# Block-sorted attention and a gated feed-forward on one Trainium2 core: the first two units' scores computed a second time transposed, later transposes by DMA, batch 0 in halves

## The chip, the core and the metric

One core of a Trainium2 chip runs the whole program. Its engines are TensorE (PE in the profile, its weight loads PEld), VectorE (DVE), ScalarE (ACT), GpSimd (POOL) and SyncE (SP), which only issues DMAs here; POOL issues the loads that turn fp32 into bf16. The metric is device time in microseconds (us), the median over runs. All times below are us unless a unit stands with them.

## What is computed

Inputs are q, k and v of 4 batches x 8 heads x 768 rows x 64, a matrix of 8x8 per head (sort_net), and three weight matrices (512x1536, 512x1536, 1536x512). All are fp32; the output is 3072x512, fp32.

```
P = sort_net
for _ in range(5):                      # per head, 8x8
    P = exp(P - max(P, axis=-1)); P = P / (sum over the row + 1e-9); P = P / (sum over the column + 1e-9)
k_sorted[i] = sum_j P[i, j] * k_block[j]        # blocks of 96 rows, the same for v
scores = q_block @ k_sorted_block.T / 8         # 96x96, block by block
attn   = exp(scores - rowmax); attn = attn / (rowsum + 1e-9)
x      = attn @ v_sorted_block                  # to 3072 tokens x 512
g = x @ w_gate
out = (g * sigmoid(g) * (x @ w_val)) @ w_out
```

## The kernel before

**Units.** Half a batch (4 blocks of 96 rows, all 8 heads) is a unit: 384 tokens, eight units. Heads are handled as four head pairs hp: head hp on partitions 0 to 63 and head hp+4 on 64 to 127 (x is 0 or 1).

**Preparation per batch.** q is loaded (line 92) and transposed on TensorE in three pieces of 16 transposes (q_piece, line 130). K is mixed by P and transposed in one step: `mix_t` (lines 134 to 143) multiplies K as it was loaded by a block-diagonal matrix bdk, made of P, in six pieces of 16 small matmuls. V of batches 1 to 3 is mixed by one 128x512 matmul a piece (v_piece, line 169), six a batch, and brought into the layout that attention needs through DRAM: written to vscr (line 177) and read back (line 179). V of batch 0 goes by `mix_t` and 32 TensorE transposes (v0_turn, line 160). ACT moves most pieces from PSUM to SBUF (evict, line 120).

**Attention of a unit, per head pair.** qk (line 251): eight matmuls into PSUM tile s (96x768). rowmax and shift on VectorE (lines 257, 262), expo on ACT (267), rowsum and reciprocal on VectorE (271, 272), norm on POOL (278), which gives en in bf16; turn (285): eight TensorE transposes of en, moved by ACT to et; av (298): eight matmuls with V, moved by ACT into xt, the input of the feed-forward part.

**Feed-forward (FFN) of a unit.** Twelve steps m, each for 128 of the 1536 hidden columns: four matmuls g and four u (line 318) of 128x384, tanh on ACT (328), gs = (tanh+1)*g and h = u/2*gs on VectorE (332, 338). Every third h of unit 0 goes another way: ACT copies u (335), POOL multiplies (336). ffn_down (346) turns three chunks of h into part of an output tile of 128x512; ACT copies it (350), SP stores it (351).

**Order.** The program is written in one order per engine by hand (manual_schedule). Up to the first FFN step it is a list (`first`, lines 399 to 404). From there each action has a time in slots, `at(t, ...)`, and is emitted in the order of these times: slot 12u+m holds step m of unit u's FFN, with a quarter of an output tile of unit u-1 at +0.5. The attention of unit u runs beside the FFN of the two units before: `att_steps` starts head pair hp at slot 12u-15.6+3hp, with turn 4 and av 5 slots later (lines 303 to 310). Batch 1 is prepared in unit 0's slots, batch 2 in slots 12 to 29, batch 3 in slots 36 to 53. Each engine takes its instructions strictly in that order, so a wait holds all that stands behind it.

**PSUM.** Eight banks: three rotate for g and u ("up"), one for output tiles ("o"), two for one score tile ("s"), two for all the rest ("m").

Of the kernel before, what the change touches and what calls it, by code (L numbers as in the profile page):

```python
# [9 lines left out]
FP32 = mybir.dt.float32  # L10
# [7 lines left out]
def kernel(  # L18
# [15 lines left out]

    nc = tc.nc
# [18 lines left out]
    CC = BLK // CQ  # L58

# [10 lines left out]
    dramp = ctx.enter_context(tc.tile_pool(name="dramp", bufs=2, space=bass.MemoryType.DRAM))  # L70
    psum = ctx.enter_context(tc.tile_pool(name="psum", bufs=2, space=bass.MemoryType.PSUM))

    def ps_tile(shape, dt, name, tag):
        return psum.tile(shape, dt, name=name, tag=tag, bufs={"up": 3, "o": 1, "s": 1, "m": 2}[tag])

    ctx.enter_context(tc.manual_schedule())


# [5 lines left out]
    def load_k(b):  # L84
        kn[b] = natp.tile([128, CK, D], BF16, name="kn", tag="kn", bufs=2)
        src = k[b].rearrange("h (j ch c) d -> (h j ch) c d", j=NB, ch=CH)
        nc.gpsimd.dma_start(out=kn[b], in_=src)

    def load_q(b):
        qn[b] = natp.tile([128, 2, CC, D], BF16, name="qn", tag="qn", bufs=2)  # L90
        src = q[b].rearrange("(x hp) (j cq c) d -> (hp j cq) x c d", x=2, j=NB, cq=CQ)
        nc.gpsimd.dma_start(out=qn[b], in_=src)

    def load_v(b):
        vn[b] = natp.tile([128, CK, D], BF16, name="vn", tag="vn", bufs=2)
        src = v[b].rearrange("h (j ch c) d -> (h j ch) c d", j=NB, ch=CH)
        nc.gpsimd.dma_start(out=vn[b], in_=src)
# [5 lines left out]

    p_sb = const.tile([BH, NB + 1, NB], FP32, name="p_sb")
    nc.sync.dma_start(out=p_sb[:, 0:NB, :], in_=sort_net.rearrange("b h i j -> (b h) i j"))
    load_q(0)
    load_k(0)
    load_v(0)
    load_w(wg_sb, moe_w_gate, 0, DF // 2)

    ident = const.tile([128, 128], BF16, name="ident")
    make_identity(nc, ident)
    load_w(wv_sb, moe_w_val, 0, DF // 2)

# [9 lines left out]
    def q_piece(b, n, eng, tag):  # L124
        if n == 0:
            tr["q", b] = trp.tile([128, HP, NB, BLK], BF16, name="qt", tag="qt")
        ps = ps_tile([128, 8, 128], BF16, "q_ps", tag)
        for l in range(8):
            for x in range(2):
                nc.tensor.transpose(ps[ds(64 * x, 64), l, :], qn[b][:, x, n * 8 + l, :], ident)  # L130
        dst = tr["q", b].rearrange("p hp i (cq c) -> p (hp i cq) c", cq=CQ)
        evict(eng, dst[:, :, ts(n, 8)], ps.transpose([0, 2, 1]))

    def mix_t(nat, b, dst, n, eng, tag):

        ps = ps_tile([128, 8, 64], FP32, "k_ps", tag)
# [330 lines left out]
```

## Time and profile before

| | |
|---|---|
| median of 3 runs (lowest to highest) | 286.16 (285.83 to 286.68) |
| profiled execution, first to last instruction (span) | 284.0 |
| around the span, median less span | 2.2 |
| first FFN matmul | 36.36 |
| first FFN matmul of units 1, 2, 3 | 66.10, 98.43, 128.41 |
| of units 4, 5, 6, 7 | 160.17, 190.15, 218.84, 246.59 |
| last output tile stored (issue) | 281.08 |
| loads that turn fp32 into bf16, in what lands | 14.16 MB |

The profiled execution's own time is given as its span only; what lies around the span is taken to be that of the median run. The profile's busy times of TensorE are those of pipelined matmuls whose ends are modelled, so the price of a group is read from the start of one to the start of the next. PEclk is the share of TensorE's full clock that was granted. Idle time of an engine that does not set the pace costs nothing. In a row of windows stand start and end, length, then busy time and count of PE, PEld, DVE, ACT and POOL, the granted clock, the share of time that the DMA engines were busy, and GB/s. In a row of the timeline: start, busy time, engine, line, operation, tiles written and read, shapes, count, and in brackets the wait before it.

### The profile page before, as it was taken

The numbers are of one execution on the slowest core, as the hardware profiler recorded it, in microseconds if no ns is written. First come the engines' busy times: TensorE is split into PE (matmuls) and PEld (weight loads), VectorE is DVE, ScalarE is ACT, GpSimd is POOL, SyncE is SP. The second block draws the span as 40 slices with busy tenths as digits, with TensorE's granted clock in tenths as the row PEclk, the third lists the DMA queues.
The fourth block names the chain that finished last, engine by engine and source line by source line (L and its number), as shares of the span: only waits on it lengthen the run. The fifth ranks groups of instructions, "written<-read, shape, count | busy, mean of one in ns | idle before, by whom it ended". The sixth has DMA issues, their size and how long they took to land.

```text
span 284.0 us, 6237 instructions
## 1 busy us (share of the span) xinstructions
PE 258.5 (91%) x2550; PEld 154.6 (54%) x2550; DVE 204.0 (72%) x360; ACT 164.3 (58%) x291; POOL 70.3 (25%) x98
## 2 busy tenths in 40 slices
PE   0577789989999999999999999999999999999983
PEld 0566645655556665555555655555555555555531
DVE  5789577749778777888887777888888887556500
ACT  2568779885766767546666666554555445432311
POOL 8155362433332222222211222222222222000000
PEclk9955589999999999999999999999999999999999
DMA  6999999997399911001039100101000010000021
GB/s 105 216 206 221 204 203 197 268 207 75 51 227 244 111 39 38 10 31 39 28 137 133 39 2 37 40 0 39 38 37 2 37 39 37 18 22 37 37 76 74
DMA packets 28412, 25.57 MB, mean 90 GB/s; under 512 B 19296, under 2 KB 22880, under 8 KB 28384
## 3 DMA queue, kind: packets, MB, share of 16 engines
q0 software_dynamic: 5968, 14.16, 26.7%
q1 hardware_dynamic: 22416, 11.02, 15.9%
q8 instruction: 20, 0.33, 0.5%
q14 instruction: 8, 0.07, 0.1%
HBM read 30.68 MB, written 8.65 MB: 138 GB/s over the span
## 4 chain that ended last, share of the span: by engine, by line
PE 65%; DVE 15%; ACT 12%; issue 4%; DMA 2%; DVEq 0%; ACTq 0%; POOLq 0%
PE o_ps L346 19%; PE g_ps L318 17%; PE u_ps L318 14%; DVE e L262 5%; DVE rm L257 5%; PE av_ps L298 3%; ACT et L120 3%; PE k_ps L139 3%; ACT e L267 3%; PE et_ps L285 2%; DMA qn<-in_q_dram 2%; ACT th L328 2%; PE s L251 2%; DVE gs L332 2%; DVE h L338 2%
## 5 line engine op out<-in xcount | busy, mean ns | idle before, releaser
L278 POOL TENSOR_TENSOR en<-e,rs 96x384 bf16<-96x384 f32 x63 | 50.9, 827 | 145.3 <-DVE rs L272 113.1
L332 DVE SCALAR_TENSOR_TENSOR gs<-th,g_ps 128x384 bf16<-128x384 bf16 x96 | 52.2, 544 | 42.5 <-ACT th L328 42.5
L346 PE MATMUL o_ps<-wo_sb,h 128*128 128x512 bf16 x288 | 76.8, 380 | 2.3 <-ACT o_sb L350 2.0
L318 PE MATMUL u_ps<-xt,wv_sb 128*128 128x384 bf16 x384 | 78.3, 327 | 0.6 <-DVE gs L332 0.5
L318 PE MATMUL g_ps<-xt,wg_sb 128*128 128x384 bf16 x384 | 78.8, 328 | 0.0
L328 ACT ACTIVATE th<-g_ps 128x384 bf16<-128x384 f32 x96 | 47.1, 490 | 53.9 <-PE g_ps L318 52.6
L338 DVE SCALAR_TENSOR_TENSOR h<-u_ps,gs 128x384 bf16<-128x384 f32 x92 | 51.3, 557 | 9.9 <-PE o_ps L346 0.5
L318 PEld LDWEIGHTS <-wg_sb 128*128 128x128 bf16 x384 | 36.9, 98 | 35.1 <-issue 2.0
L318 PEld LDWEIGHTS <-wv_sb 128*128 128x128 bf16 x384 | 37.7, 98 | 26.1 <-issue 1.6
L267 ACT ACTIVATE e<-e 96x768 f32<-96x768 f32 x32 | 27.0, 843 | 19.3 <-DVE e L262 19.3
L346 PEld LDWEIGHTS <-h 128*128 128x128 bf16 x288 | 23.9, 98 | 22.9 <-issue 3.1
L262 DVE TENSOR_TENSOR e<-s,rm 96x768 f32<-96x768 f32 x32 | 30.5, 954 | 2.8
L257 DVE TENSOR_REDUCE rm<-s 96x8 f32<-96x768 f32 x32 | 30.2, 943 | 2.8 <-PE s L251 2.7
L271 DVE TENSOR_REDUCE rs<-e 96x8 f32<-96x768 f32 x32 | 30.0, 938 | 1.3 <-ACT e L267 1.3
L120 ACT COPY et<-et_ps 96x768 bf16<-96x768 bf16 x32 | 25.0, 781 | 1.7 <-PE et_ps L285 1.7
L350 ACT COPY o_sb<-o_ps 128x512 f32<-128x512 f32 x24 | 14.0, 585 | 16.8 <-PE o_ps L346 16.7
L285 PEld LDWEIGHTS <-en 96*96 96x96 bf16 x256 | 17.4, 133 | 3.2
L285 PE MATMUL et_ps<-ident,en 96*96 96x96 bf16 x256 | 18.1, 217 | 0.0
L120 ACT CAST xt<-av_ps 128x384 bf16<-128x384 f32 x32 | 15.3, 477 | 4.4 <-PE av_ps L298 3.6
L130 PE MATMUL q_ps<-ident,qn 128*64 128x128 bf16 x192 | 8.5, 244 | 9.0 <-DMA qn<-in_q_dram 8.0
L298 PEld LDWEIGHTS <-vt 96*64 96x64 bf16 x256 | 9.4, 114 | 11.8 <-issue 11.3
L298 PE MATMUL av_ps<-et,vt 96*64 96x96 bf16 x256 | 12.2, 218 | 3.8 <-ACT et L120 3.3
(54 smaller groups left out, 154.3 us busy)
## 6 DMA issues: line engine op xcount, KB each, us to landing
out_dram<-o_sb SPq DMA_DIRECT2D x24, 256.0 KB, 2.0
qn<-in_q_dram POOLq DMA_DIRECT2D x4, 768.0 KB, 10.0
kn<-in_k_dram POOLq DMA_DIRECT2D x4, 768.0 KB, 10.4
vn<-in_v_dram POOLq DMA_DIRECT2D x4, 768.0 KB, 13.3
vscr<-vm SPq DMA_DIRECT2D x3, 768.0 KB, 6.7
vt<-vscr SPq DMA_DIRECT2D x3, 768.0 KB, 8.3
wg_sb<-in_moe_w_gate_dram POOLq DMA_DIRECT2D x4, 384.0 KB, 15.8
wv_sb<-in_moe_w_val_dram POOLq DMA_DIRECT2D x4, 384.0 KB, 18.1
```

The lines of the kernel that those rows point to most:

```text
L120: nc.scalar.copy(dst, src)
L257: nc.vector.reduce_max(m[:, :, :, 0], st["s", u, hp], axis=AX.X)
L262: nc.vector.tensor_tensor(e, st["s", u, hp], st["m", u, hp].to_broadcast([BLK, 2, HB, BLK]), op=ALU.subtract)
L267: nc.scalar.activation(st["e", u, hp], st["e", u, hp], AF.Exp, scale=scale)
L278: engs[x].tensor_tensor(st["en", u, hp][:, x], st["e", u, hp][:, x], st["rs", u, hp][:, x].to_broadcast([BLK, HB, BLK]), op=ALU.mult)
L285: nc.tensor.transpose(ps[:, x * HB + i, :], st["en", u, hp][:, x, i, :], ident[0:BLK, 0:BLK])
L298: nc.tensor.matmul(ps[ds(64 * x, 64), i, :], lhsT=tr["v", b][:, (x * HP + hp) * NB + i0 + i, :], rhs=st["et", u, hp][:, x, i, :], start=Tr ...
L318: nc.tensor.matmul(ps, lhsT=w_sb[:, kc, ts(m, 128)], rhs=xt[u][:, kc, :], start=(kc == 0), stop=(kc == HP - 1))
L328: nc.scalar.activation(st["th"], st["g"], AF.Tanh, scale=0.5)
L332: nc.vector.scalar_tensor_tensor(gs, st["th"], 1.0, st["g"], op0=ALU.add, op1=ALU.mult)
L338: nc.vector.scalar_tensor_tensor(h_t[u][:, m, :], st["u"], 0.5, gs, op0=ALU.mult, op1=ALU.mult)
L346: nc.tensor.matmul(st["o"], lhsT=h_t[u][:, m, ts(t, 128)], rhs=wo_sb[:, m, :], start=(m == 0), stop=(m == NFC - 1))
```

## The change

- **Scores of units 0 and 1 twice.** qk as before gives maxima (t_max, VectorE), which TensorE turns (t_maxt) and ACT copies; then t_st computes the scores again, transposed, and takes the maxima off by a second matmul with a constant matrix (selm); t_exp goes straight from PSUM to bf16 on ACT. Nothing is turned afterwards. The row sums are matmuls with ones (t_av), and t_div divides after av: reciprocal on VectorE, then the product on VectorE or, for two head pairs of unit 0 and all of unit 1, by an ACT copy and POOL. shift, rowsum, norm and turn fall away for these units.
- **Transposes by DMA.** From unit 2 on, turn is one DMA transpose from SP of en (padded to 128 columns a block). q of batches 2 and 3 is loaded in another layout by eight DMAs a batch (load_qd) and turned by four DMAs (qd_turn). V of batches 1 to 3 is mixed by 16 small matmuls a piece, as K is, and turned by two DMAs (v_flip); the way through DRAM is gone. V of batch 0 is still turned on TensorE. (v0_flip is defined and not called.)
- **Batch 0 in halves.** q is loaded in two halves of pieces of three rows; q, K and V are prepared for unit 0 first, K and V with matmuls half as wide and twice as many (mix_half, v0_piece); unit 1's K follows ahead of the first FFN step, its q and V in unit 0's slots.
- **Joined visits.** av of a head pair stands just ahead of qk of a later one in the same slot (6.05 and 0.1); a V and a K piece of batches 2 and 3 stand together, every third slot, in slots 16 to 31 and 40 to 55.
- **h over ACT and POOL.** Every second h up to step 8, then two of three, instead of every third in unit 0 alone (via_pool).
- **Banks.** PSUM banks are named by hand; the last three output tiles rotate over four banks ("oo ua ub uc"). Weights are loaded in thirds.

The diff, cut:

```diff
-    def ps_tile(shape, dt, name, tag):
-        return psum.tile(shape, dt, name=name, tag=tag, bufs={"up": 3, "o": 1, "s": 1, "m": 2}[tag])
...
+    sa = psum.tile([128, 2, 512], FP32, name="sa_ps")
+    bank = {n: psum.tile([128, 512], FP32, name=f"{n}_ps") for n in ("ma", "mb", "ua", "ub", "uc", "oo")}
...
+    def ps(group, shape, dt=FP32, parts=128):
+        turns[group] = turns.get(group, -1) + 1
+        names = group.split()
+        t = bank[names[turns[group] % len(names)]]
...
+    UP, MM = "ua ub uc", "ma mb"
...
+    def load_q0(half):
...
+    def load_qd(b, x):
+        if x == 0:
+            qd[b] = natp.tile([BLK, NB, HP, 2, D], BF16, name="qd", tag="qn", bufs=2)
+        for hp in range(HP):
+            nc.gpsimd.dma_start(out=qd[b][:, :, hp, x, :],
+                                in_=q[b][x * HP + hp].rearrange("(i c) d -> c i d", i=NB))
...
+    def q0_piece(half, n, eng, group):
...
+        for l in range(6):
+            hp, c = 2 * n + l // CC0, l % CC0
+            for x in range(2):
+                nc.tensor.transpose(p[ds(64 * x, 64), l, :], qn[0, half][:, x * HP + hp, c, :], ident)
...
+    def qd_turn(b, part):
...
+        n = NB // 4
+        nc.sync.dma_start(out=tr["qx", b][:, ts(part, n)].rearrange("p i hp c -> p (i hp) c"),
+                          in_=qd[b][:, ts(part, n)].rearrange("c i hp x d -> c (i hp x d)"),
+                          transpose=True)
+    def mix_half(nat, half, dst, n, eng, group):
+        p = ps(group, [16, 32])
+        for l in range(16):
+            for x in range(2):
+                nc.tensor.matmul(p[ds(64 * x, 64), l, :], lhsT=nat[:, n * 16 + l, :],
+                                 rhs=bdk[:, 0, ds(HP * x, HP), ds(half * HB, HB)],
+                                 start=True, stop=True)
+        evict(eng, dst[:, :, ts(n, 16)], p.transpose([0, 2, 1]))
...
-    def v_piece(b, n, eng, tag):
...
-        ps = ps_tile([128, 8, D], FP32, "v_ps", tag)
-        nc.tensor.matmul(ps.rearrange("p c d -> p (c d)"),
-                         lhsT=bdk[:, b].rearrange("p h i c -> p (h i c)"),
-                         rhs=vn[b][:, ts(n, 8), :].rearrange("p c d -> p (c d)"),
-                         start=True, stop=True)
-        evict(eng, tr["vm", b][:, ts(n, 8), :], ps)
-    def v_turn(b):
...
-        nc.sync.dma_start(out=scr.rearrange("hi (ch c) d -> (hi ch) c d", ch=CH), in_=tr["vm", b])
-        tr["v", b] = trp.tile([BLK, H * NB, D], BF16, name="vt", tag="vt")
-        nc.sync.dma_start(out=tr["v", b], in_=scr.rearrange("hi c d -> c hi d"))
...
+    def v0_piece(half, n, eng, group):
...
+        evict(eng, dst[:, :, :, ts(n, 16)], p.rearrange("p l (g ch) -> p g ch l", ch=CH))
+    def v_piece(b, n, eng, group):
...
+        p = ps(group, [8, 64])
+        for l in range(8):
+            for x in range(2):
+                nc.tensor.matmul(p[ds(64 * x, 64), l, :], lhsT=vn[b][:, n * 8 + l, :],
+                                 rhs=bdk[:, b, ds(HP * x, HP)].rearrange("p a i c -> p (a i c)"),
+                                 start=True, stop=True)
+        evict(eng, dst[:, :, :, ts(n, 8)], p.rearrange("p l (g ch) -> p g ch l", ch=CH))
+    def v0_turn(half, n, eng, group):
...
+        for g in range(8):
+            nc.tensor.transpose(p[:, g, :], vpad[:, half * 16 + n * 8 + g, 0:BLK], ident)
...
+    def v_flip(b, part, parts=2):
...
+        n = HP * NB // parts
+        nc.sync.dma_start(out=tr["vb", b][:, ts(part, n), :],
+                          in_=vpad[:, ts(part, n), :].rearrange("p g c -> p (g c)"), transpose=True)
...
+    def qk_mm(out, u, hp):
+        for i in range(HB):
+            for x in range(2):
+                r = ds(64 * x, 64)
+                nc.tensor.matmul(out[x][:, ts(i, BLK)], lhsT=tr["q", u][r, hp, i, :],
+                                 rhs=tr["k", u][r, hp, i, :], start=True, stop=True)
...
+    def t_qk(u, hp, pair):
+        st["s", u, hp] = [bank[n] for n in pair.split()]
+        qk_mm([t[0:BLK] for t in st["s", u, hp]], u, hp)
+    def halves(u, hp):
+        s = st["s", u, hp]
+        if s[0] is bank["na"]:
+            return [(slice(0, 2), sa[0:BLK, :, 0:UT])]
+        return [(slice(x, x + 1), s[x][0:BLK, 0:UT].unsqueeze(1)) for x in range(2)]
+    def t_max(u, hp):
+        m = rmb[hp]
+        for x, s in halves(u, hp):
+            nc.vector.reduce_max(m[:, x, 0:HB], s.rearrange("p x (i c) -> p x i c", i=HB), axis=AX.X)
+        st["m", u, hp] = m
+    def t_maxt(u, hp, eng):
+        p = st["s", u, hp][0][:, UT:UT + BLK // 2].bitcast(BF16)
+        nc.tensor.transpose(p, st["m", u, hp].rearrange("p x i -> p (x i)"), ident[0:BLK, 0:BLK])
+        mt = smp.tile([128, BLK], BF16, name="mt", tag="mt")
+        evict(eng, mt, p)
+        st["mt", u, hp] = mt
+    def t_st(u, hp):
+        for i in range(HB):
+            for last in range(2):
+                for x in range(2):
+                    r = ds(64 * x, 64)
+                    nc.tensor.matmul(st["s", u, hp][x][0:BLK, ts(i, BLK)],
+                                     lhsT=selm[r, i, :] if last else tr["k", u][r, hp, i, :],
+                                     rhs=st["mt", u, hp][r, :] if last else tr["q", u][r, hp, i, :],
+                                     start=not last, stop=bool(last))
+    def t_exp(u, hp):
+        et = epool.tile([BLK, 2, HB * BLK], BF16, name="ett", tag="ett", bufs=3)
+        for x, s in halves(u, hp):
+            nc.scalar.activation(et[:, x], s, AF.Exp, scale=scale)
+        st["et", u, hp] = et
+    def t_av(u, hp, av, den):
+        new_xt(u)
+        av, den = ps(av, [UT]), ps(den, [UT])
+        et = st["et", u, hp]
+        for x in range(2):
+            nc.tensor.matmul(den[ds(64 * x, 64), :], lhsT=ones, rhs=et[:, x, :], start=True, stop=True)
+        for i in range(HB):
+            for x in range(2):
+                nc.tensor.matmul(av[ds(64 * x, 64), ts(i, BLK)],
+                                 lhsT=tr["v", u][0:BLK, hp, i, ds(64 * x, 64)],
+                                 rhs=et[:, x, ts(i, BLK)], start=True, stop=True)
+        st["av", u, hp] = av, den
+    def t_div(u, hp, eng):
+        av, den = st["av", u, hp]
+        r = smp.tile([128, UT], FP32, name="rden", tag="rden", bufs=2)
+        nc.vector.reciprocal(r, den)
+        if eng == "dve":
+            nc.vector.tensor_tensor(xt[u][:, hp, :], av, r, op=ALU.mult)
+        else:
+            x = smp.tile([128, UT], FP32, name="xu", tag="xu", bufs=2)
+            nc.scalar.copy(x, av)
+            nc.gpsimd.tensor_tensor(xt[u][:, hp, :], x, r, op=ALU.mult)
+    ens = [epool.tile([BLK, 2 * HB, 128], BF16, name=f"en{n}", tag=f"en{n}", bufs=1) for n in range(3)]
...
+    def norm(u, hp):
+        en = ens[(u * HP + hp) % 3]
...
         for x in range(2):
...
+            nc.gpsimd.tensor_tensor(en[:, ds(x * HB, HB), 0:BLK], st["e", u, hp][:, x],
+                                    st["rs", u, hp][:, x].to_broadcast([BLK, HB, BLK]), op=ALU.mult)
     def turn(u, hp):
-        ps = ps_tile([BLK, 2 * HB, BLK], BF16, "et_ps", "m")
-        for x in range(2):
-            for i in range(HB):
-                nc.tensor.transpose(ps[:, x * HB + i, :], st["en", u, hp][:, x, i, :],
-                                    ident[0:BLK, 0:BLK])
...
+        et = epool.tile([128, 2 * HB, BLK], BF16, name="et", tag="et", bufs=3)
+        nc.sync.dma_start(out=et, in_=st["en", u, hp].rearrange("p g c -> p (g c)"), transpose=True)
         st["et", u, hp] = et
...
+        p = ps(MM, [HB, BLK])
...
+    def via_pool(u, m):
+        s = NFC * u + m
+        return s % 2 == 1 if s < 9 else s % 3 < 2 if s < 20 else s % 3 != 1
...
-            nc.scalar.activation(u_sb, st["u"], AF.Copy, scale=0.5)
-            nc.gpsimd.tensor_tensor(h_t[u][:, m, :], u_sb, gs, op=ALU.mult)
...
+        if via_pool(u, m):
...
+            nc.scalar.activation(st["us", u, m], st["u", u, m], AF.Copy, scale=0.5)
...
+    def ffn_h(u, m):
+        if via_pool(u, m):
+            nc.gpsimd.tensor_tensor(h_t[u][:, m, :], st["us", u, m], st["gs", u, m], op=ALU.mult)
...
-            st["o"] = ps_tile([128, DM], FP32, "o_ps", "o")
+            st["o"] = ps(group, [DM])
...
+    for n, (eng, b) in enumerate([("act", "oo"), ("dve", "ua"), ("act", "ub")]):
+        k0_piece(0, n, eng, b)
...
+    v0_piece(0, 0, "act", "ma")
+    v0_piece(0, 1, "act", "mb")
+    t_qk(0, 0, "na nb")
+    t_max(0, 0)
+    t_qk(0, 1, "ua ub")
+    t_max(0, 1)
+    t_qk(0, 2, "uc oo")
+    t_max(0, 2)
+    t_maxt(0, 0, "act")
+    v0_piece(0, 2, "act", "ma")
+    t_st(0, 0)
+    t_maxt(0, 1, "act")
+    t_exp(0, 0)
+    t_qk(0, 3, "ma mb")
+    t_max(0, 3)
+    t_st(0, 1)
+    t_maxt(0, 2, "act")
+    t_exp(0, 1)
+    v0_turn(0, 0, "dve", "na")
+    t_st(0, 2)
+    t_maxt(0, 3, "act")
+    t_exp(0, 2)
+    t_st(0, 3)
+    v0_turn(0, 1, "dve", "ua")
+    t_exp(0, 3)
+    t_av(0, 0, "ub", "uc")
+    t_div(0, 0, "pool")
+    t_av(0, 1, "na", "nb")
+    t_div(0, 1, "pool")
+    t_av(0, 2, "ua", "oo")
+    t_div(0, 2, "dve")
+    t_av(0, 3, "ma", "mb")
+    t_div(0, 3, "dve")
+    k0_piece(1, 0, "act", "uc")
+    k0_piece(1, 1, "act", "oo")
+    k0_piece(1, 2, "act", "na")
...
+    for t, f, args in [
+            (1.0, v0_piece, (1, 0)), (1.0, v0_piece, (1, 1)), (2.0, v0_piece, (1, 2)), (3.0, v0_turn, (1, 0)),
+            (5.0, v0_turn, (1, 1)), (4.0, k_piece, (1, 0)), (4.9, k_piece, (1, 1)), (5.0, k_piece, (1, 2)),
+            (6.0, k_piece, (1, 3)), (6.9, k_piece, (1, 4)), (7.0, k_piece, (1, 5)), (5.9, q_piece, (1, 0)),
+            (7.4, q_piece, (1, 1)), (8.0, q_piece, (1, 2)), (8.9, v_piece, (1, 0)), (9.0, v_piece, (1, 1)),
+            (9.9, v_piece, (1, 2)), (10.0, v_piece, (1, 3)), (10.4, v_piece, (1, 4)), (10.9, v_piece, (1, 5))]:
+        st["n"] = st.get("n", 0) + 1
+        at(t + 0.1, f, *args, ("act", "dve")[st["n"] % 2], P3 if t < 11.4 else MM)
+    for part in range(2):
+        at(11.2 + 0.1 * part, v_flip, 1, part)
+    for hp in range(HP):
+        t = 1 + 2 * hp
+        for dt, f, args in [(0.2, t_qk, ("na nb",)), (0.35, t_max, ()), (1.05, t_maxt, ("act",)), (1.2, t_st, ()),
+                            (1.95, t_exp, ()), (3.07, t_av, (P3, P3)), (3.35, t_div, ("pool",))]:
+            at(t + dt, f, 1, hp, *args)
...
+    for x in range(2):
+        at(20.0 + 4 * x, load_qd, 2, x)
+        at(41.0 + 4 * x, load_qd, 3, x)
...
+        t = 24 * b + T0
+        for n in range(6):
+            at(t - 16 + 3 * n + 0.05, v_piece, b, n, "act", MM)
+            at(t - 16 + 3 * n + 0.06, k_piece, b, n, "act", MM)
+        for part in range(2):
+            at(t + 0.1 * part, v_flip, b, part)
+        for part in range(4):
+            at(t - 6 + part, qd_turn, b, part)
+    for u in range(2, NU):
+        t0 = 12 * u + T0 + (u == 2)
+        for hp in range(HP):
+            for dt, f in [(0.1, qk), (0.35, rowmax), (0.45, shift), (1.6, expo), (2.1, rowsum), (2.12, recip),
+                          (2.3, norm), (2.4, turn), ((5.05 if u == 2 else 6.05) - 0.07 * (hp == 3), av)]:
+                at(t0 + 3 * hp + dt, f, u, hp)
...
-        at(12 * NU + t, ffn_down, NU - 1, t, 0, 1)
...
+        at(12 * NU + t, ffn_down, NU - 1, t, 0, 1, "oo " + UP)
```

## The prediction

> **What bounds the kernel.** The page's busy shares and slices come first:
>
> ```profile
> PE 258.5 (91%) x2550; PEld 154.6 (54%) x2550; DVE 204.0 (72%) x360; ACT 164.3 (58%) x291; POOL 70.3 (25%) x98
> ...
> PE   0577789989999999999999999999999999999983
> ...
> PEclk9955589999999999999999999999999999999999
> DMA  6999999997399911001039100101000010000021
> ```
>
> TensorE is full from about 36 us on, and before that neither full nor at its clock. The windows by unit, cut where the first g_ps matmul of each unit of the feed-forward part (FFN) starts, say how long each lasts:
>
> ```profile
> 36.36:66.10 29.74, 26.63 (x336) 16.41 (x335) 20.85 (x34) 23.55 (x43) 12.02 (x15) 0.97 1.16 214
> 66.10:98.43 32.33, 32.26 (x339) 18.63 (x338) 26.03 (x44) 21.57 (x41) 10.70 (x14) 1.00 0.81 145
> ...
> 190.15:218.84 28.69, 28.39 (x230) 16.20 (x228) 24.04 (x41) 15.03 (x27) 6.43 (x8) 1.00 0.08 29
> ```
>
> So units 1 to 6 are TensorE's own work; the units between last 29.98, 31.76, 29.98, and unit 6 27.75. The timeline of TensorE gives the price of each visit, read from start to start (busy times overlap):
>
> ```profile
> 191.45 0.52 PE L285 MATMUL et_ps<-ident,en 96*96 96x96 bf16 x8
> 191.81 0.81 PE L346 MATMUL o_ps<-wo_sb,h 128*128 128x512 bf16 x3
> 192.46 0.81 PE L318 MATMUL g_ps<-xt,wg_sb 128*128 128x384 bf16 x4
> 193.10 0.81 PE L318 MATMUL u_ps<-xt,wv_sb 128*128 128x384 bf16 x4
> 193.96 0.36 PE L298 MATMUL av_ps<-et,vt 96*64 96x96 bf16 x8
> 194.26 0.82 PE L346 MATMUL o_ps<-wo_sb,h 128*128 128x512 bf16 x3
> ```
>
> A slot (g, u and a third of o) is 3x0.65 = 1.95. The turn costs 0.36. av costs 0.30 and another 0.21 between u_ps and it (193.10 to 193.96 is 0.86, not 0.65); qk costs 0.31 and 0.09. Three slots with one head pair of attention: 5.85+0.36+0.51+0.40 = 7.12; the chain repeats at 7.13. The waits and the windows of the start show two more places:
>
> ```profile
> PE o_ps L346 <- ACT o_sb L350: 2.0, 3, 0.7
> ...
> 17.50:20.90 3.40, 2.42 (x74) 2.06 (x68) 2.68 (x4) 3.00 (x6) 2.44 (x4) 0.50 1.15 206
> ...
> 34.60:38.00 3.40, 3.40 (x30) 2.21 (x26) 2.57 (x4) 2.06 (x5) 1.53 (x2) 0.50 1.16 212
> 38.00:41.40 3.40, 2.51 (x21) 1.53 (x20) 2.56 (x5) 3.17 (x6) 1.63 (x3) 1.00 1.10 210
> ```
>
> The last tiles wait for one PSUM bank, and the clock stays at 0.50 from 14.1 on until TensorE was busy for 3.40 of 3.40 us.
>
> **Basis.** The span is 284.0; the median of the runs is 286.16, so 2.2 lie around it. The profiled execution has no other time; I sum from 284.0+2.2.
>
> **Units 1 to 7.** Units 2 to 7 of attention lose the turn (-0.36 each), batches 2 and 3 lose six q pieces (0.57 each, 59.98 to 60.55). Against that a V piece, one matmul of 0.22 (73.12 to 73.34), becomes 16 small ones like a K piece, 0.37 (83.35 to 83.73). Joining av and qk saves the 0.09 of the second visit. In qk right after av (88.56 to 88.86 is 0.30) there is no extra. So three slots become 5.85+0.21+0.30+0.31 = 6.67; a V and a K piece together, in a visit of their own, add 0.84. Head pair 3's av comes 0.07 slots early, ahead of the slot's g, so it isn't joined: 0.90, not 0.81.
> - Unit 1: 23.4 for 12 slots, five qk and four av (3x0.40+2x0.51+0.81+0.90 = 3.9), three V-K visits (2.5): 29.9, by 2.4 less.
> - Units 2 and 4: 23.4+3.3+2.5 = 29.3, by 0.7 less each. Unit 3, which had V and K pieces: 29.3, by 2.5 less.
> - Unit 5: 26.8, by 1.9 less. Unit 6 (two qk, four av): 26.1, by 1.65 less.
> - Tail: four banks in turn instead of one end the three waits of 0.67: 2.0 less.
> Sum: -11.9.
>
> Who else could be late there? Per three slots VectorE needs 3 gs (0.54), one h (0.56, the other two go to POOL), and 0.94+0.95+0.94+0.20: 5.2 of 6.7. ACT: 3 tanh, 2 copies of u (0.49 each), 0.84, 0.48, a share of o_sb 0.44: 4.2, with two pieces 5.4 of 7.5. POOL: norm 1.61 and two h at 0.91: 3.4. Sums fit, but one order is tight: rowsum and reciprocal now stand ahead of the third gs, which ends about 7.25 after the first g starts (th after expo at 6.0, rowsum and reciprocal to 6.7), while u of the next slot needs its bank at 7.33. Bounds 0 to 0.2 each over 20 cycles; I take +0.5 in all.
>
> **The turn by DMA.** No row shows a DMA transpose. norm ends about 8.4 into its cycle (rowsum to 6.5, reciprocal to 6.7, POOL 1.6); av comes two cycles after its qk, at 14.9. That leaves 6.5. The DMA moves 96 rows of 2 KB, 192 KB in 768 rows of 256 B. The nearest rows are in the page's list of DMA issues (KB each, us to landing):
>
> ```profile
> out_dram<-o_sb SPq DMA_DIRECT2D x24, 256.0 KB, 2.0
> ...
> vscr<-vm SPq DMA_DIRECT2D x3, 768.0 KB, 6.7
> vt<-vscr SPq DMA_DIRECT2D x3, 768.0 KB, 8.3
> ```
>
> Their ends, 2.0 and 8.3 (four times the bytes, in pieces of 128 B), are my bounds. I take 3.5, nearest to out in bytes and above it for its smaller pieces: hidden. Behind it on SP only outputs and other transposes queue. The two V flips of batch 1 (0.5 MB each, at slot 11) stand ahead of unit 2's first turn; two times the vscr row's 6.7 would be 13.4 of the about 8 there, a stall once of 0 to 6; I take 0.5. The V round trip through DRAM goes, and with it most packets of the hardware queue. load_qd issues eight DMAs a batch on POOL, in fours at 0.55 to 0.8 each: 3.2 in POOL's queue ahead of a norm, within its window.
>
> [...]
>
> **The start.** The Sinkhorn chain is untouched; pbf is there at 11.8, and K pieces start at 13.0, as now (ACT evicts only one q piece ahead of the last exp, worth 0.2). 96 K matmuls of half the width: the full ones went at 24 ns each, 2.29; if that is issue, half width is no faster, so 15.3. Then two V pieces (64 at 31 ns, 2.0) to 17.3, where the old kernel began qk at 16.0. From there nothing waits for a shift: three qk (0.49 at half clock) have their own banks; VectorE does only maxima (about 1.0 each), reciprocal and some divisions, instead of 3.0 per head pair. TensorE has work without a gap from 15.3, so the window 17.5 to 20.9 is full and by the row above the clock comes at about 21. [...]
> Worked forward: second scores (16 matmuls: 1.0 at half clock, 0.65 at full) end at 21.1, 22.35, 23.65, 24.95, each behind ACT's copy of the maxima and the last exp; exps (0.85 to 1.0) end at 22.5, 23.95, 25.25, 26.25; V turns are evicted by 26.6; av with the sums (0.55) ends at 27.75; VectorE's four reciprocals and two products (0.55 each) at 29.9; TensorE's K pieces for half 1 at 30.0. FFN starts at 30.0 instead of 36.36. If the clock stays at half, the same order is TensorE's own, 18.9 from 15.3: 34.2. The reciprocal of 128x384 has no row: 0.54 as other 384-wide operations, or up to 1.85 by the 4 ns an element above the fixed 0.16 that 96x8 in 0.199 allows; that end adds 2.6 here.
>
> **Unit 0's slots.** TensorE: 12 x 1.31 = 15.7; q 0.86, V half 96x23 ns = 2.25 and turns 0.8, K 2.25, q 1.7, V 2.25 of batch 1; unit 1's qk, maxima, second scores, av with sums: 6.2; unit 2's qk 0.3. That is 32.5, and about 2 of visits: 34.5. ACT comes to 24, VectorE to 27, so they fit, but three banks serve 31 uses; waits were 3.1 of 29.74 before, and I take 1.5: 36. So unit 1 starts at 66.0, where it was 66.10: what the start wins, the transposed scores spend. Loads: the slices show 0.21 MB a us. K and V of batch 0 with the first half of q are 2.0 MB, 9.4 after the first 2; q's pieces of 384 B may add 2: V is there at about 14, before 15.3. All weights and batch 1's K are 4 MB more: by about 36, before slot 8 needs the last.
>
> **Sum.** 286.2-0.1-11.9+0.5+0.5 = 275.2; I say 275, and 270 to 280 for this case.
>
> **Rivals.**
> 1. The clock stays at 0.50 until the FFN, or batch 1's pieces wait for banks: start at 34.2 and slots at half clock for 1 to 2 more: +4 to +8, 279 to 284. For it: 14.1 to 17.5 was busy 2.71 of 3.40 and got no clock. Against: there are no gaps left.
> 2. The turn by DMA is late (**slower**): its tiles go one after another. Place: av waits for et. av comes two cycles and 1.5 after its qk's cycle began, so 8.4+d = 2 cycles+1.5: from d = 6.5 on every us costs 0.5 per cycle over some 22 cycles, 11 us; d = 7.5 is no change, the vt row's 8.3 gives 295. For it: no row shows that a transpose is spread over the engines. Against: the hardware queue's 22416 packets took 15.9% of 16 engines' span, 32 ns each and many at once, and DMA slices are at 0 to 1 after 96 us.
> 3. The opening is lighter: half-wide matmuls cost half (-4 over K and V halves), waits vanish: 265 to 270.
> 4. The joined visits save nothing: 24x0.09 = 2 more; inside the forecast's range.
>
> **Numbers.** Forecast 0.62, first rival 0.14, second 0.16 (a sixth of it between 6.5 and 7.5, still faster), third 0.08. The range 267 to 286 leaves out most of the second and the end of the third. Faster by over 0.3% (what a measurement of this kernel tells from no change): 0.62+0.14+0.08 and 0.01 of the second, 0.85; within: 0.02 of it; slower: its remaining 0.13.
>
> **What would show it.** Three slots at 6.7 without waits of av for et; et landing in under 6.5; the granted clock at 1.00 by about 21 and FFN's start near 30; unit 1's start near 66; no wait of o_ps for o_sb. A wait of TensorE for a DMA of et, or VectorE full in unit 0, would make it wrong.

## The result and the profile after

The changed kernel takes 304.3 (median of 4 runs, 300.74 to 305.39) beside 286.42 (285.83 to 287.01) of the kernel before: 1.058 times as long (95% interval 1.051 to 1.064). Forecast were 275 and a range of 267 to 286, so sign and range are both wrong. A run more than 1.5% longer than the fastest of its kernel counts as slow, and all ratios here leave such runs out, while the medians of times hold them. The profiled execution took 303.69, its span is 301.9.

First the busy shares and slices of the changed kernel:

```profile
PE 258.5 (86%) x2785; PEld 152.0 (50%) x2812; DVE 185.9 (62%) x300; ACT 157.2 (52%) x307; POOL 135.8 (45%) x178
...
PE   0487389978682999999978999999999999999995
...
PEclk9999556999985799999997999999999999999999
DMA  7999899000099319989993996457721332210012
```

TensorE is busy for the same 258.5 as before, in a span that is 18 longer: the time went into gaps. The deepest lie in slices 5 (counted from 1), 9 to 13 and 21, and the clock is low in or just behind slices 5, 13 and 21. The DMA row is another as well: transfers fill most slices from 16 to 29, where the old kernel had little but 0 and 1 (apart from slices 21 and 22).

The windows of units 0, 1, 2, 3 and 5 (cut where each unit's first g matmul starts; columns as before) say which units are long:

```profile
35.88:82.65 46.77, 39.03 (x627) 25.45 (x625) 35.27 (x44) 23.15 (x43) 12.46 (x17) 0.83 0.43 79
82.65:122.88 40.23, 32.68 (x296) 17.26 (x300) 20.69 (x34) 18.77 (x37) 19.30 (x25) 0.84 0.77 111
122.88:151.38 28.50, 28.08 (x290) 15.94 (x293) 20.39 (x33) 19.09 (x37) 17.86 (x23) 1.00 1.04 145
151.38:184.51 33.13, 29.77 (x290) 16.56 (x293) 20.38 (x33) 19.21 (x37) 19.80 (x25) 0.95 0.84 110
213.00:239.91 26.91, 26.14 (x194) 14.43 (x197) 20.29 (x33) 15.97 (x31) 13.74 (x17) 1.00 0.32 62
```

| | forecast | after |
|---|---|---|
| first FFN matmul | 30.0 | 35.88 |
| unit 0 | 36.0 | 46.77 |
| unit 1 | 29.9 | 40.23 |
| unit 2 | 29.3 | 28.50 |
| unit 3 | 29.3 | 33.13 |
| unit 4 | 29.3 | 28.49 |
| units 5, 6 | 26.8, 26.1 | 26.91, 26.19 |
| unit 7 and tail | 35.4 | 35.8 |

Units 2 and 4 to 7 came out within 0.9 of the forecast. All that was lost is in the start (5.9), unit 0 (10.8), unit 1 (10.3) and unit 3 (3.8). The waits of TensorE name two releasers. The forecast had the wait for the first at nothing, and VectorE's work behind the second (rden, the reciprocal) at a fifth of its time:

```profile
PE ma_ps L474 <- DMA et<-en: 9.5, 2, 6.5
...
PE oo_ps L199 <- DVE rden L418: 4.1, 1, 4.1
```

**At the start** it is VectorE. Its timeline up to the first FFN step:

```profile
26.64 2.54 DVE L418 RECIPROCAL rden<-uc_ps 128x384 f32<-128x384 f32 x1
29.10 2.49 DVE L418 RECIPROCAL rden<-sa_ps 128x384 f32<-128x384 f32 x1
31.51 2.49 DVE L418 RECIPROCAL rden<-oo_ps 128x384 f32<-128x384 f32 x1
34.52 0.56 DVE L420 TENSOR_TENSOR xt<-ua_ps,rden 128x384 bf16<-128x384 f32 x1 [0.52 <-DVE rden L418]
35.00 2.55 DVE L418 RECIPROCAL rden<-mb_ps 128x384 f32<-128x384 f32 x1
```

One reciprocal of 128x384 takes 2.5, beside 0.56 for a product of the same size: four in a row are 10, and TensorE's K pieces for unit 1 wait behind them for banks (1.32 and 4.14). Four more stand in unit 0's slots. Clock is lost as well: the granted clock falls to 0.50 at 30.39 and comes back at 50.87, in the midst of unit 0, where TensorE is busy for 39.03. In e3 below, without the reciprocal, the clock is low from 30.83 to 34.24 (0.53 in the mean of 30.60 to 34.00) and TensorE is busy for 35.33 in unit 0.

**In unit 1** it is a DMA. The timeline of TensorE around the longest wait:

```profile
88.77 0.81 PE L485 MATMUL uc_ps<-xt,wv_sb 128*128 128x384 bf16 x4
96.11 0.53 PE L474 MATMUL ma_ps<-et,vt 96*64 96x96 bf16 x8 [6.52 <-DMA et<-en]
96.57 1.46 PE L520 MATMUL oo_ps<-wo_sb,h 128*128 128x512 bf16 x3
97.83 1.49 PE L485 MATMUL ua_ps<-xt,wg_sb 128*128 128x384 bf16 x4
```

av stands and waits for its turned e, and what comes behind it runs at half clock (0.50 granted from 96.11 to 101.00): four matmuls of 128x384 show 1.49 where they showed 0.81. The list of DMAs issued from 80 to 104 (median us to landing at the end; the transposes carry no size) shows what the turn met:

```profile
vn<-in_v_dram POOLq DMA_DIRECT2D x1, 768.0 KB, 8.4
kn<-in_k_dram POOLq DMA_DIRECT2D x1, 768.0 KB, 9.3
out_dram<-o_sb SPq DMA_DIRECT2D x1, 256.0 KB, 2.0
vt<-vpad SPq DMA_TRANSPOSE x2, 7.5
et<-en SPq DMA_TRANSPOSE x2, 9.3
```

The first of the two turns was issued at 87.35 and landed at 96.07; the V load of batch 2 ran from 86.79 to 95.22. Later turns with no load beside them land in 2.8 (the expectations below have 2.65 for this). In unit 3 the wait is 2.9, and the trace of SP shows how: the issue of the second V flip of batch 2 lasts from 149.35 to 156.57, beside the K load of batch 3 (147.72 to 156.79), and the turn behind it is issued at 156.69.

Three theories follow: the reciprocal, the loads beside the turns, and, as the loads' rival, the V flips that stand ahead of these turns on SP.

### The profile page after: what moved, and what is told of

Same layout as the page of the kernel before. It is cut to its first block, busy times and chain, and to the rows that moved or that the text cites. A ratio compares the mean times of both kernels' runs of the same rounds, so it can differ in the third digit from the quotient of the medians.

```text
span 301.9 us, 6981 instructions
## 1 busy us (share of the span) xinstructions
PE 258.5 (86%) x2785; PEld 152.0 (50%) x2812; DVE 185.9 (62%) x300; ACT 157.2 (52%) x307; POOL 135.8 (45%) x178
## 3 DMA queue, kind: packets, MB, share of 16 engines
q0 software_dynamic: 20864, 14.16, 33.7%
q1 hardware_dynamic: 41584, 15.74, 26.1%
## 4 chain that ended last, share of the span: by engine, by line
PE 71%; DVE 13%; DMA 5%; ACT 4%; issue 3%; POOL 2%; SPq 1%; DVEq 0%; POOLq 0%; ACTq 0%
PE oo_ps L520 17%; PE ub_ps L485 13%; PE ua_ps L485 13%; PE uc_ps L485 11%; DMA et<-en 5%; DVE rden L418 4%; PE sa_ps L353 3%; SPq L272 1%; DVE rs L451 1%; PE mb_ps L474 1%; POOL en L461 1%; PE ma_ps L474 1%; DVE gs L506 1%; PE ma_ps L235 1%; ACT e L447 1%
## 5 line engine op out<-in xcount | busy, mean ns | idle before, releaser
L510 POOL TENSOR_TENSOR h<-u_sb,gs 128x384 bf16<-128x384 f32 x63 | 57.4, 913 | 88.7 <-ACT u_sb L502 72.1
L520 PE MATMUL oo_ps<-wo_sb,h 128*128 128x512 bf16 x237 | 68.5, 388 | 2.9 <-issue 1.4
L485 PE MATMUL ua_ps<-xt,wg_sb 128*128 128x384 bf16 x128 | 28.9, 351 | 1.3 <-DVE xt L420 1.2
L485 PE MATMUL ub_ps<-xt,wv_sb 128*128 128x384 bf16 x128 | 28.2, 346 | 0.0
L485 PE MATMUL uc_ps<-xt,wv_sb 128*128 128x384 bf16 x128 | 27.3, 337 | 0.9 <-DVE gs L506 0.9
L485 PE MATMUL ua_ps<-xt,wv_sb 128*128 128x384 bf16 x128 | 26.7, 332 | 0.7 <-DVE gs L506 0.5
L485 PE MATMUL ub_ps<-xt,wg_sb 128*128 128x384 bf16 x128 | 26.8, 333 | 0.1
L485 PE MATMUL uc_ps<-xt,wg_sb 128*128 128x384 bf16 x128 | 26.7, 332 | 0.1
L438 DVE TENSOR_REDUCE rm<-sa_ps 96x8 f32<-96x768 f32 x24 | 22.8, 952 | 5.5 <-PE sa_ps L353 4.9
L443 DVE TENSOR_TENSOR e<-sa_ps,rm 96x768 f32<-96x768 f32 x24 | 22.9, 953 | 0.8
```

The source lines that it names most:

```text
L438: nc.vector.reduce_max(m[:, :, :, 0], s4(u, hp), axis=AX.X)
L443: nc.vector.tensor_tensor(e, s4(u, hp), st["m", u, hp].to_broadcast([BLK, 2, HB, BLK]), op=ALU.subtract)
L485: nc.tensor.matmul(p, lhsT=w_sb[:, kc, ts(m, 128)], rhs=xt[u][:, kc, :], start=(kc == 0), stop=(kc == HP - 1))
L510: nc.gpsimd.tensor_tensor(h_t[u][:, m, :], st["us", u, m], st["gs", u, m], op=ALU.mult)
L520: nc.tensor.matmul(st["o"], lhsT=h_t[u][:, m, ts(t, 128)], rhs=wo_sb[:, m, :], start=(m == 0), stop=(m == NFC - 1))
```

## The experiments

### The reciprocal, the loads, and both

e1 takes the reciprocal away, e2 moves the loads, e3 does both. Without the reciprocal units 0 and 1 are multiplied by their row sums instead of divided, so e1 and e3 give a time and no usable output.

```diff
 e1, e3
-        nc.vector.reciprocal(r, den)
+        nc.vector.tensor_copy(r, den)
 e2, e3
-        kn[b] = natp.tile([128, CK, D], BF16, name="kn", tag="kv", bufs=3)
+        kn[b] = natp.tile([128, CK, D], BF16, name="kn", tag="kv", bufs=4)
...
-        vn[b] = natp.tile([128, CK, D], BF16, name="vn", tag="kv", bufs=3)
+        vn[b] = natp.tile([128, CK, D], BF16, name="vn", tag="kv", bufs=4)
...
-    at(13.0, load_v, 2)
-    at(14.5, load_k, 2)
+    at(2.6, load_v, 2)
+    at(4.6, load_k, 2)
...
-    at(30.0, load_v, 3)
-    at(34.0, load_k, 3)
+    at(23.8, load_v, 3)
+    at(26.9, load_k, 3)
```

> The changed kernel, with the eight 128x384 reciprocals replaced by copies of the same shape; so the output is multiplied by the row sums of units 0 and 1 instead of divided, and only the time is read. Theory (each reciprocal costs 2.55 instead of 0.54 and holds VectorE in the start and in unit 0): the FFN starts near 30 instead of 35.9, unit 0's slots take about 37 instead of 46.8, units 1 and 3 stay at 40 and 33: about 289. Rival (unit 0 is long because three PSUM banks serve 31 uses): the start wins 6, unit 0 stays at 44 or more: about 297.

> The changed kernel, with a fourth buffer for K and V as loaded, and the loads of V and K of batches 2 and 3 moved from slots 13, 14.5, 30 and 34 to 2.6, 4.6, 23.8 and 26.9. Theory (a DMA transpose beside a load ends only when the load does): the first turns of unit 2 land in 3 to 5 instead of 8.5 and 9.7, the window from unit 1's first FFN matmul to unit 2's is about 30 instead of 40, unit 3 29.5 instead of 33: about 290. Rival (the turns wait behind the two V flips in SP's queue, whatever the loads do): unit 1 stays at 38 or more: 300 to 304.

> Both edits of the two runs before at once (units 0 and 1 are multiplied by their row sums). If these two costs are all that the forecast lacked: 275 to 279, with the FFN's start near 30, unit 0 near 37 and unit 1 near 30. If banks or something else holds the slots of unit 0: 285 or more.

Measured medians: e1 295.7 (ratio to before 1.0175, 1.0135 to 1.0215), e2 289.76 (1.0104, 1.0076 to 1.0131), e3 280.12 (0.9764, 0.9739 to 0.9788). Beside the changed kernel's ratio of 1.0576 the reciprocal alone is worth 4.0% of the old kernel's time (11.5), the loads alone 4.7% (13.5), both together 8.1% (23.3). That turns the sign: e3 is faster than the kernel before. e2 came out as forecast (290). e1 was forecast at 289 and e3 at 275 to 279: both took longer.

e2 keeps the V flips of batch 1 ahead of unit 2's first turn. Its DMAs from 78 to 92:

```profile
vt<-vpad SPq DMA_TRANSPOSE x2, 6.0
et<-en SPq DMA_TRANSPOSE x2, 2.9
```

Without a load in flight the same turns behind the same flips land in 2.9 and not 9.3, and unit 3 is 28.49 for 33.13. The flips alone are not the cause; they cost a wait of 2.5 for et in unit 1 of e2, and no clock (1.00 in that unit's window, 79.59 to 112.07). e1 shows how much hangs on what meets what: with the reciprocal gone the units come earlier, unit 2's first turns meet both loads, and the wait of TensorE in unit 1 grows (in a profiled execution of 298.63):

```profile
PE ma_ps L474 <- DMA et<-en: 15.2, 1, 15.2
```

Two other executions of e1 took 290.44 and 292.77, so the wait need not be that long in each.

e3 has neither loss, and starts the FFN at 30.76 (forecast 30.0). But its unit 0 is still long. Windows of units 0 and 1 of e3:

```profile
30.76:70.79 40.03, 35.33 (x624) 23.36 (x624) 26.40 (x44) 23.21 (x44) 15.77 (x23) 0.93 0.78 143
70.79:102.01 31.22, 29.34 (x296) 16.21 (x300) 20.32 (x34) 18.77 (x37) 17.88 (x23) 0.98 0.64 89
```

Forecast for unit 0 were 34.5 of TensorE's work and 1.5 of waits. It is 35.33 busy and 4.7 of gaps (the waits named: banks that ACT's copies and VectorE's gs still hold, 2.0 and 1.2 the largest). Unit 1 is 31.22, with waits for et of 0.9 and 0.3.

### The tail's banks alone

```diff
-        at(12 * NU + t, ffn_down, NU - 1, t, 0, 1)
+        at(12 * NU + t, ffn_down, NU - 1, t, 0, 1, "up")
```

> The kernel before, with one part of the change alone: the last three output tiles rotate over the three banks of g and u instead of waiting for the one of the output. Theory: the three waits of 0.67 go, 2.0 less than the kernel before. Rival (the end is set by the last store, which comes as late): no difference.

284.27, ratio 0.9914 (0.9898 to 0.9930): 2.0 to 2.9 less. The term stands. (Here the tiles rotate over the three banks of g and u; the changed kernel uses four.)

### The parts from unit 2 on, with the old units 0 and 1

e5 is the kernel before, with the changed kernel's units 2 to 7. Its core:

```diff
     at(2.1, load_v, 2)
     at(5.1, load_k, 2)
-    at(7.1, load_q, 2)
-    at(15.1, load_v, 3)
-    at(17.1, load_k, 3)
-    at(19.1, load_q, 3)
+    at(6.1, load_v, 3)
+    at(8.6, load_k, 3)
...
+    for u in range(2, NU):
+        t0 = 12 * u - 16 + (u == 2)
+        for hp in range(HP):
+            for dt, f in [(0.1, qk), (0.35, rowmax), (0.45, shift), (1.6, expo), (2.1, rowsum), (2.12, recip),
+                          (2.3, norm_p), (2.4, turn_d), ((5.05 if u == 2 else 6.05) - 0.07 * (hp == 3), av)]:
+                at(t0 + 3 * hp + dt, f, u, hp)
```

> Units 0 and 1 are prepared as in the kernel before (shift, row sum, turn on TensorE, no division of 128x384); from unit 2 on everything is as after the change (et, q and V turned by DMA, joined visits, most h over ACT and POOL, output tiles of the tail on four banks), and all V and K loads are issued by slot 8.6, ahead of the first turn at slot 11.4. Theory (the parts from unit 2 on gain what was forecast; only the division in units 0 and 1 and the loads beside turns lose): unit 2 starts at 96 to 98.5, where the kernel before had it (98.4), and from there the sequence of the changed kernel without stalls, 28.5+28.5+28.5+26.9+26.2+35.8 = 174.4: a span of 271 to 273, a time of 273 to 275. Rival (turns by DMA, flips and qd turns cost something even without loads beside them): unit 2 or 3 over 30, a time of 278 or more.

275.69 (273.73 to 279.75), ratio 0.9598 (0.9542 to 0.9655). Units 2 to 6 are 28.49, 28.50, 28.49, 26.91 and 26.19, to a few hundredths those of the changed kernel where nothing stalls. The times scatter over 6.0, and the profiled execution is the longest, 279.75: its unit 1 lasts 37.07, with two waits for et of 2.3 and 2.2, and half clock for 3.4 behind each (four matmuls of 128x384 show 1.49 and 1.48 there, for 0.81). The shorter executions need not have these waits.

e6 puts the loads back to their late slots, and e7 puts the turn of e back on TensorE, two slots later:

```diff
 e6
-    at(2.1, load_v, 2)
-    at(5.1, load_k, 2)
-    at(6.1, load_v, 3)
-    at(8.6, load_k, 3)
+    at(13.0, load_v, 2)
+    at(14.5, load_k, 2)
+    at(30.0, load_v, 3)
+    at(34.0, load_k, 3)
 e7
+        ps = ps_tile([BLK, 2 * HB, BLK], BF16, "et_ps", "m")
+        for g in range(2 * HB):
+            nc.tensor.transpose(ps[:, g, :], st["en", u, hp][:, g, 0:BLK], ident[0:BLK, 0:BLK])
...
-        nc.sync.dma_start(out=et, in_=st["en", u, hp].rearrange("p g c -> p (g c)"), transpose=True)
+        evict("act", et[0:BLK], ps)
...
-                          (2.3, norm_p), (2.4, turn_d), ((5.05 if u == 2 else 6.05) - 0.07 * (hp == 3), av)]:
+                          (2.3, norm_p), (4.4, turn_d), ((5.05 if u == 2 else 6.05) - 0.07 * (hp == 3), av)]:
```

> The hybrid with one thing put back: V and K of batches 2 and 3 are loaded at slots 13.0, 14.5, 30.0 and 34.0, as in the changed kernel, so that each is in flight beside turns. Theory (a turn by DMA that shares the engines with a load takes 8 to 10 us instead of 2.65): TensorE waits for et in unit 1 and in unit 3, two stalls of 3 to 7 us, 6 to 10 us more than the hybrid: 280 to 284. Rival (the stall of the changed kernel came from the two V flips of batch 1 in SP's queue, which this kernel doesn't have): at most 2 us more than the hybrid, and a turn beside a load still lands in under 5 us.

> The hybrid with e of units 2 to 7 turned on TensorE again (eight transposes and one copy by ACT for a head pair); q and V of batches 2 and 3 still go by DMA. Theory (the turn by DMA saves TensorE's own time, 0.36 us for each of 24 head pairs, and nothing else): 8.6 us more than the hybrid, 282 to 284. Rival (ACT was what kept the slots long and gets 24 copies of about 0.9 back): 12 us more or beyond. Other rival (the gain comes from h over POOL, and the turn is hidden anyway): within 3 us of the hybrid.

e6: 286.15, ratio 0.9994 (0.9969 to 1.0019), by the ratios 11.3 more than e5. That is a little over the theory's 6 to 10, and the place is only half of it. TensorE in unit 1 of e6:

```profile
78.82 0.44 PE L203 MATMUL v_ps<-bdk,vn 128*64 128x64 bf16 x16 [1.29 <-DMA vn<-in_v_dram]
83.86 0.64 PE L148 MATMUL k_ps<-bdk,kn 128*64 128x64 bf16 x16 [4.59 <-DMA kn<-in_k_dram]
```

Here it was not av that waited, but the V and K pieces of slot 16, for their own loads. A turn issued at 75.18 beside the K load took until 84.47, with no flip in SP's queue, but nobody needed it sooner. In unit 3 the wait was for et, 2.5, and the unit was 32.73. So e6 speaks for the theory by the landings, and not by its time; e10 below mends that.

e7: 284.37, ratio 0.9922 (0.9897 to 0.9946), by the ratios 9.3 more than e5, which looks like the forecast's 24 x 0.36 = 8.6 and isn't quite that. In units 2 to 6 alone, where e5 has no stall, e7's 147.3 beside 138.6 are 8.7 for 20 head pairs, 0.44 each; the other four stand in unit 1, where e5's profiled execution has its stalls. The timeline of unit 5 shows the turn's own 0.36 (191.31 to 191.67) and a u matmul that starts 0.25 later in its slot; what it waits for was not found. With e4's 284.27 beside it: as long as the turn is on TensorE, all the other parts together (q and V by DMA, joined visits, h over POOL, earlier loads) are worth nothing that can be measured.

### A version that beats both

```diff
-    at(6.1, load_v, 3)
-    at(8.6, load_k, 3)
+    at(4.6, load_v, 3)
+    at(6.6, load_k, 3)
...
-        at(20.0 + 4 * x, load_qd, 2, x)
-        at(41.0 + 4 * x, load_qd, 3, x)
+        at(19.45 + 5 * x, load_qd, 2, x)
+        at(40.45 + 4 * x, load_qd, 3, x)
...
-        t0 = 12 * u - 16 + (u == 2)
+        t0, gap = (8.8, 2.75) if u == 2 else (12 * u - 16, 3)
...
-                          (2.3, norm_p), (2.4, turn_d), ((5.05 if u == 2 else 6.05) - 0.07 * (hp == 3), av)]:
-                at(t0 + 3 * hp + dt, f, u, hp)
+                          (2.3, norm_p), (2.4, turn_d), ((5.8 if u == 2 else 6.05) - 0.07 * (hp == 3), av)]:
+                at(t0 + gap * hp + dt, f, u, hp)
```

> The hybrid with three moves and no other change: V and K of batch 3 are issued at slots 4.6 and 6.6 (not 6.1 and 8.6), so that the last has landed before the first turn; the four POOL issues of q of batch 2 stand behind the last norm of unit 2, not ahead of it; and unit 2's head pairs start 2.75 slots apart from slot 8.8 on, with av 5.8 slots behind (not 3 apart and 5.05). Theory (what is left over the forecast in unit 1 of the hybrid, two waits for et of about 2.3 us in the profile, the first beside a K load in flight, the second because unit 2's av comes a slot earlier than the others', each with some 2 us at half clock behind it): unit 1 at 29.5 to 31 instead of 37 in the hybrid's profile, the time 271 to 273.5. Rival (unit 1 is TensorE's own work at about 32, as before, and the waits only take its place): within 1 us of the hybrid's fast runs, 273.7 to 275.

273.09 (273.04 to 273.18), ratio 0.9529 (0.9501 to 0.9556): faster than the kernel before by 4.7%, and faster than the changed one by a tenth. Windows of units 0, 1 and 2:

```profile
36.71:67.50 30.79, 27.20 (x344) 16.59 (x343) 21.16 (x34) 24.05 (x44) 12.42 (x16) 0.97 1.10 215
67.50:97.05 29.55, 28.10 (x291) 15.96 (x293) 21.09 (x35) 19.23 (x38) 19.30 (x24) 1.00 0.59 83
97.05:125.55 28.50, 28.08 (x290) 15.94 (x293) 20.21 (x33) 18.96 (x37) 16.73 (x21) 1.00 0.80 128
```

Unit 1 is 29.55 at a full clock (forecast for the changed kernel 29.9). The rest of its wait for et is 0.9, once. The scatter of e5 went with the waits. Which of the three moves did how much was not told apart.

### h over ACT and POOL

```diff
-        return m % 3 == 2 if u == 0 else (s >= 12 and (s % 3 < 2 if s < 20 else s % 3 != 1))
+        return m % 3 == 2 if u == 0 else False
```

> The early hybrid (273.1) with h of units 1 to 7 all on VectorE again, from u in PSUM, and no copy of u by ACT; nothing else is changed. Theory (by the sums of the prediction VectorE then has three gs, three h and 3.03 us of softmax in three slots, 0.54x3+0.56x3+3.03 = 6.3 of 6.67: it fits, but gs comes late behind the row sum, and a bank with it): 0.1 to 0.3 us in each of 24 cycles, 2 to 7 us more, 275 to 280. Rival (TensorE is the bound and VectorE's share is hidden, so that moving h to ACT and POOL bought nothing): within 1 us of 273.1. Other rival (VectorE is the bound): as long as VectorE's own sum, 10 us more or beyond.

273.62, ratio 0.9543 (0.9517 to 0.9570), not to be told from e8. Unit 2 of e9 (unit 3 has the same busy times of TensorE, VectorE and ACT):

```profile
97.00:125.50 28.50, 28.50 (x300) 15.94 (x296) 23.56 (x41) 15.85 (x29) 8.59 (x11) 1.00 0.86 128
```

VectorE is busy for 23.56 of 28.50 instead of 20.21, and from the start of unit 2 on no slot moves by more than 0.02. The theory (a late gs) falls, its rival holds: TensorE is the bound, and moving h bought nothing here.

### Turns beside a load, with no flip near

```diff
-    at(4.6, load_v, 3)
-    at(6.6, load_k, 3)
+    at(22.25, load_v, 3)
+    at(25.25, load_k, 3)
```

> The early hybrid (273.1) with one thing put back: V and K of batch 3 are issued at slots 22.25 and 25.25, just ahead of the turns at 22.4 and 25.4, and no piece needs them before slot 40, so that nothing but turns can wait; no V flip stands near. (With the loads of the earlier hybrid put late, 5.9 of the loss in unit 1 were V and K pieces that waited for their own loads, which this kernel leaves out.) Theory (beside a load a turn takes 5 to 10 us, and unit 3's av comes about 8 us behind the issue of its turn): those two turns land in 5 to 10 us, TensorE waits for et by 0 to 3 us at each, with up to 2.5 us at half clock behind a wait: 1 to 6 us more, 274 to 279. Rival (a turn is slow only behind another transpose in SP's queue): both turns land in under 3.5 us, within 0.5 us of 273.1.

278.07 (275.54 to 279.3), ratio 0.9687 (0.9624 to 0.9750): 5 more than e8, from two loads moved. The turn beside the V load landed in 6.2 (95.99 to 102.22) and its av did not wait; the one beside the K load in 8.4 (105.21 to 113.58; the load from 102.96 to 112.70). e8's two landed in 2.6 and 3.0, with the same small q loads in flight. Then TensorE, and the window of that unit:

```profile
113.63 0.53 PE L360 MATMUL av_ps<-etd,vt 96*64 96x96 bf16 x8 [3.41 <-DMA etd<-en]
```

```profile
96.84:131.64 34.80, 30.96 (x289) 16.91 (x292) 20.19 (x33) 19.21 (x37) 17.31 (x22) 0.90 0.96 149
```

The wait is 3.41, the unit 6.3 longer than e8's 28.50; the other 2.9 are at the lower clock, 0.90 in the mean. This late DMA cost TensorE about twice what the wait shows. No other transpose was in flight ahead of either turn, so the rival falls.

The DMA queues also show what the turn met. Queue q1 carries what SP issues, and q0 what POOL issues (its 14.16 MB in the changed kernel are all of POOL's loads). This is all that moved on the two from the second turn's issue to 109.00 (packets, MB, share of the 16 engines' time; a q load's packets are among them until 105.8):

```profile
q0 software_dynamic: 196, 0.56, 93.5%
```

The turn had no packet on the way for 3.8, where e8's had its first 1.2 behind the issue. From 109.00 to its landing q1 has 94.6% (the next turns of q on it too) and q0 21.1%. So the turn did not share the engines with the load from the start: it stood until the load's packets thinned out.

## Why the prediction was wrong, step by step

- **The reciprocal (failed step: "0.54 as other 384-wide operations, or up to 1.85").** It takes 2.55, beyond the bound as well. The row that the bound came from, 96x8 in 0.199, was read with a fixed cost of 0.16 (an estimate: of the kernel before, h with 384 columns in 0.557 and e with 768 in 0.954 give 2x0.557-0.954 = 0.16), and the sum does not come out: (0.199-0.16)/8 is 4.9 ns an element, which makes 2.03 and not 1.85. With 2.548 for 384 elements the two rows give (2548-199)/(384-8) = 6.2 ns an element. Eight are 20.4 of VectorE instead of 4.3. By the ratios e1 prices it at 11.5, and e3 beside e2 at 9.7; in the profiles of e2 and e3 this is 5.6 at the start (36.35 and 30.76) and 3.2 in unit 0.
- **The turn by DMA (failed step: "hidden", with the DMA slices "at 0 to 1 after 96 us").** Undisturbed, its 2.8 is under the 3.5 that was taken; beside loads it was 8.7 and 9.9, past the 6.5 that the order left, and TensorE waited for two turns of 24 (6.5 and 2.9). These ran beside a load, or behind a flip that did. The slices were those of the kernel before; the change itself moves V and K of batches 2 and 3 from slots 2.1, 5.1, 15.1 and 17.1 to 13, 14.5, 30 and 34, between the turns. The second rival named the right place (av waits for et) and the wrong condition (late in all cycles; that the tiles go one after another no run shows). By the ratios e2 prices the loads at 13.5, and e10 shows them alone: 6.2 and 8.4 beside a load, where e8 has 2.6 and 3.0.
- **The flip's stall (+0.5).** With the loads away it is 2.5 in e2: a small miss. The four POOL issues of q (3.2, "within its window") were a small one too: in e5 they stand from 90.03 to 93.18 ahead of a norm whose reciprocal was ready at 92.47, which is 0.7 late; the turn behind it took 4.5 beside these q loads, and unit 2 has a slot less of window.
- **The half clock behind a wait** stood only in the first rival, for the start. It doubled the stall of 3.41 in e10, and came behind waits of 2.3 and 2.2 in e5, but not behind the 2.50 of e2, where the matmuls that follow keep their 0.81 (granted clock 1.00).
- **The start.** All of it but the reciprocal held: the clock came at 23.57 (forecast about 21) and stayed until 30.39, the last av there ended at about 27.9 (forecast 27.75); e3 starts the FFN at 30.76. (The clock's record begins at 23.57, and the 9s that the PEclk row shows ahead of it are no measurement: 32 K matmuls took 0.83 from start to start at 12.92, as at 34.06 under a recorded 0.50, and 0.51 in e3 at 29.59 under 1.00.) The forecast read from one row that a stretch of 3.40 busy for 3.40 brings the clock; in the changed kernel 44.20 to 47.60 is as full at 0.50, and the clock is back only at 50.87.
- **Unit 0.** TensorE's own work 35.33 in e3 (forecast 34.5); the waits, taken at 1.5, are 4.7 there. This term was mis-sized by 3.2. With division for nothing, e3 reaches unit 2 at 102.0, and e8 with the old units 0 and 1 at 97.05. The two differ in more than the second scores (batch 0 in halves, V of batch 1 by flips), so what the second scores cost by themselves was not measured.
- **Units 2 to 7 and the tail.** Right where nothing stalled. Units 2 to 6 were forecast at 7.45 less; without stalls they are 138.6 beside 148.2, 9.6 less. The tail's 2.0 was measured at 2.0 to 2.9 (e4); unit 7 with the tail of the changed kernel is 35.8 beside 37.45, 1.6 less. The late gs (+0.5) did not show (e9). The sum spread the gain over several parts; by e7 and e4 most of the 13.5 that e8 gains is the turn (about 9) and the tail (2.0 to 2.9), and by e9 none of it is h. Unit 1, forecast at 29.9, is 31.22 in e3, with 1.2 of waits for et.

The two failed steps together are 23.3 by the ratios; of the 5 that remain from e3's 280.1 to 275, 4.0 are unit 0.

**What stays open.** e10's queues show that a turn's packets stand while a load's run (3.8 without one); why the load goes first, no run here tells. SP's own issue grows from 1.2 to as much as 5.3 beside loads (e1), so part of the delay can lie there already. The waits of unit 0 in e3 are named and were not taken away.

## What to carry to other kernels

Price each operation by a row of that operation, and where there is none, don't let the bound come from its neighbours in size (the reciprocal took 2.55, a product of that size 0.56): the price is open until it is measured. When a change leans on an idle resource, draw that resource with the change in place, moved loads included, before calling it idle. A transfer that TensorE waits for needs slack for its slow case, not for its median (9.9 and 2.8 for the turns of the changed kernel); when it is late, the lower clock behind it can cost about as much again (2.9 behind a wait of 3.41 in e10, nothing behind 2.50 in e2).

## What was not expected of the hardware

- VectorE's reciprocal took 2.55 for 128x384 (changed kernel), 4.6 times the 0.56 of a product of that size; from the 0.199 for 96x8 it grows by 6.2 ns an element.
- A DMA transpose of 96x1024 in bf16, issued from SP, lands in 2.8 with nothing beside it (2.6 in e8), in 6.2 and 8.4 beside a 768 KB load that turns fp32 into bf16 (e10), in 8.7 and 9.9 where a second such load begins before the first has landed (changed kernel), and in 16.0 in the profiled execution of e1 (77.99 to 93.98). A turn issued 1.7 ahead of a load still landed in 2.7 (e6, at 69.73). Beside small q loads (96 KB each) it landed in 2.6 (e8), 4.5 (e5) and 4.9 (changed kernel, issued at 169.11). Whether its eight tiles go one after another was not shown; if they do, each takes at most an estimated 0.35 (2.8 over eight).
- The issue of such a transpose holds SP for 1.21 when quiet, and up to 7.2 for a V flip beside a load (149.35 to 156.57 in the changed kernel; two of them took 4.71 together in e8, from 119.64), with everything behind it in SP's queue: the next turn was issued at 156.69.
